# Fused attention and two feed-forward layers on one core: where the early stores are queued, and how soon the first layer's weights are asked for and decoded

## The chip, the cores and the metric

The kernel runs on one core of a Trainium2 chip. The metric is the device time of one execution in microseconds. Before the change three executions took 1014.46, 1020.41 and 1012.8 us, median 1014.46 us.

## The reference, cut to what matters

q, k, v and f are fp32, the weights arrive as 64-bit floats and are used as fp32. Attention over 4 batches and 8 heads of 576 tokens with head dimension 64, with a causal mask and a decay from running sums of log f; its output, 2304 tokens by 512, goes through two layers:

```
scores = q @ k.T / 8 + cum[:, None] - cum[None, :]      # masked above the diagonal
x = softmax(scores) @ v                                 # 4x8x576x64 -> 2304x512
h = x @ w_in;  g = h - tanh(h);   y = g @ w_out         # 2304x512x2048x512   (first layer)
h = y @ w2_in; g = relu(h)**2;    out = g @ w2_out      # the same sizes      (second layer)
```

## The kernel before, in words

**Matmuls in three products.** A fp32 matrix is split into a high part (fp32r) and the remainder, and a product is made of high x high, high x low and low x high. So every weight and every activation has to be split by the other engines before TensorE can take it.

**Weights.** The first layer's weights come in 16 chunks. Chunk fc is `wraw_fc` (512 KB of `w_in` and 512 KB of `w_out`, two DMAs on SyncE's queue, SP, through `load()`, L139). `decode_w()` (L185) makes fp32 of the 64-bit words and splits it, each in two halves: ACT scales the two words of each number (L203, L204), DVE puts their bits together (L210, L212, four instructions a chunk), ACT copies the high part (L227), and the low part is one subtraction for each half (L228): the first half on POOL, the second on DVE. A chunk thus issues five instructions on DVE (L210 twice, L212 twice, L228 once). `w_fc` is the result; TensorE needs it for `h` (L1007: x times `w_in`) and for `y` (L1047: g times `w_out`).

**Attention.** It goes by pairs of heads and halves of the queries: scores `s` (L701, L732), masks and decay on POOL (L543, from `neg`, rows of the running sums read back from `cscr` in DRAM), softmax on DVE and ACT (`Pb`, L661, L670), transposes `pt`, products `pv`, and the results `xt`. Two heads give `xs`; `pair_done()` (L876) splits it at once for the first block of 256 tokens, else it stores it to `xscr` in DRAM with `load()`, so on SP's queue and, while the early phase lasts, kept at its place in program order.

**First layer.** It runs by blocks of 256 tokens and by pairs of chunks of the hidden dimension: `h` on TensorE, tanh on ACT (L1017), `g = h - tanh(h)` on DVE (L1020), the high part `ghl` on ACT (L1024), the low part `ghl` on DVE (L1028), then `y`. `ghl_0_s` below is that of the first block's step s; step s takes the chunks 2s and 2s+1.

**What sets the order.** Attention's first pairs run alone; from the fifth pair on, attention's atoms and the first layer's steps are mixed by their costs (the loop at L1502 and on). All deferred work goes through `Clockwork`: `cw.later(k, fn)` runs fn k steps later, with k from the table `LAG` (L57). Weights are asked for by `feed.upload(n)` and decoded by `feed.pace(n)`. In the first pairs n comes from `UP[0] + i * UP[1]` and from `FEED[0]` to `FEED[1]` chunks; in the mixed part `paced()` sets them from the position in the first layer, with `UP[2]` as a factor for the asking, and the decoding is to reach 16 chunks at `FEED[2]` of a block's cost. When all 16 chunks have been asked for, `steady` is set and `load()` no longer keeps the program order.

The functions below carry the line numbers of the profile before; after the change all lines behind L141 stand six lower in the file (L228 is L234, L1007 is L1013, L1028 is L1034, L1047 is L1053).

Of the kernel before, what the change touches and what calls it, by code (L numbers as in the profile page):

```python
# [30 lines left out]
Q0, NQ, NK = (0, 256), (256, 320), (256, 576)  # L31
# [10 lines left out]
XB = (64, 768)  # L42
RING, WIDE = 5, 3
ENDS = (0.5, 1.0, 1.8, 6.45)
UP = (2, 0.1, 1.0)
HOT = 200
SUMS = 16

# [1 line left out]
NP2 = NF // 2  # L50
L2HOT = 200

FEED, FIRST = (1, 4, 0.7), 9


FILL = {2: 8, 4: 5}
LAG = dict(max=2, exp=1, norm=3, tr=3, trlo=2, pv=1, pvadd=1, qk=1, qklo=1, th=1, sub=1, hi=1, lo=1, wbits=2, wparts=3,  # L57
           relu=1, sq=1, lo2=1, load=8)


# [49 lines left out]
def fused_kernel(ctx: ExitStack, tc: tile.TileContext, q, k, v, f, w1i, w1o, w2i, w2o, out):  # L110
    nc = tc.nc
# [9 lines left out]
    xscr = {(b, hf): dram.tile([P, ND, NQ[hf]], F32, name=f"xscr_{b}_{hf}") for b in range(B) for hf in range(2)}  # L121
    yscr = [dram.tile([P, ND, NB], F32, name=f"yscr_{j}") for j in range(NBLK)]
    cscr = dram.tile([B * H, S], F32, name="cscr")
# [11 lines left out]
    steady = []  # L135

    def load(dst, src):

        ins = nc.sync.dma_start(dst, src)  # L139
        if not steady:  # L140
            tc.keep_in_program_order(ins)  # L141

    ordered = []

# [246 lines left out]
    def sum_logs(hf, tri, row, twice=None):  # L391

        s0, m = Q0[hf], NQ[hf]
        rps = bank("a", 4, f"rps_{hf}")
        chunks = [c for c, (k0, kn) in enumerate(KC) if k0 < s0 + m]
        for c in chunks:
            k0, kn = KC[c]
            lo = max(s0, k0)
            nc.tensor.matmul(rps[:32, lo - s0 : m], lhsT=lfT[:kn, c], rhs=tri_cols(tri, kn, lo - k0, s0 + m - lo),
                             start=c == 0, stop=c == chunks[-1])  # L400
        nc.vector.tensor_scalar(row[:, :m], rps[:32, :m], -8.0, None, op0=ALU.mult)
        (nc.sync if hf else nc.scalar).dma_start(cscr[:, s0 : s0 + m], row[:, :m])
        cps = bank("a", 4, f"cps_{hf}")
        for t in [c for c in chunks if KC[c][0] >= s0]:
            k0, kn = KC[t]
            for c in range(t + 1):
                cn = KC[c][1]
                o = min(k0 - KC[c][0], P)
                x = tri[:cn, o : o + P] if kn == P or c < t else twice
                nc.tensor.matmul(cps[:, t * 32 : t * 32 + 32], lhsT=x, rhs=lfT[:cn, c], start=c == 0, stop=c == t)  # L410
            nc.vector.tensor_scalar(ccol[:, t], cps[:, t * 32 : t * 32 + 32], 8.0, None, op0=ALU.mult)

    def first_sums():
# [5 lines left out]
        load_next("v")  # L419
        feed.upload(UP[0])  # L420
        make_identity(nc, ident)
# [219 lines left out]
    def softmax_of(i):  # L641
# [13 lines left out]
        def softmax(work):  # L655
# [11 lines left out]
            def ex():  # L667
                for x, (T, parts) in enumerate(work):
                    d = pb[:rows, T[2] : T[2] + T[3]]
                    soon(i, nc.scalar.activation(d, d, AF.Exp, bias=stat(len(parts) - 1, x)[:rows], scale=-1.0,  # L670
                                                 accum_out=stat(2, x)[:rows]))
                cw.later(LAG['norm'], nrm)

# [202 lines left out]
    def pair_done(b, hf, p, xs):  # L876
        if (b, hf) == (0, 0):
            t = xhl[0][p]
            nc.scalar.activation(t[:, 0], xs[:, :NB], AF.Copy)
            nc.vector.tensor_tensor(t[:, 1], xs[:, :NB], t[:, 0].bitcast(F32), op=ALU.subtract)  # L880
        else:
            load(xscr[b, hf][:, p, :], xs[:, : NQ[hf]])

    def attn_stream():

        yield 0, first_sums, 0
        yield 0, (lambda: (decay(0), decay(1), feed.upload(UP[0]))), 0
        for c, a in kq_atom(0):
# [568 lines left out]
    for i in range(n_start):  # L1457
        cw.step(astream[i][1], HOT)
        feed.upload(int(UP[0] + i * UP[1]))
        if i >= FIRST:  # L1460
# [16 lines left out]
    def paced():  # L1477
        if feed.loaded == NF and not steady:
            steady.append(True)
        if feed.loaded < NF:  # L1480
            feed.upload(min(NF, int(loaded0 + UP[2] * (NF - loaded0) * mpos / (FEED[2] * bc))))
        feed.pace(FEED[1] + (NF - FEED[1]) * mpos / (FEED[2] * bc) if feed.decoded < NF else goal2[0])
# [54 lines left out]
```

## Time and profile before

| | us |
|---|---|
| three executions | 1012.8, 1014.46, 1020.41 |
| the profiled execution | 1012.92 |
| its span | 1011.2 |
| TensorE busy in the span | 984.8 (97%) |
| VectorE (DVE) busy | 719.8 (71%) |
| ScalarE (ACT) busy | 629.3 (62%) |
| GpSimd (POOL) busy | 347.3 (34%) |

The profiled execution's time lies 1.72 us above its span. PE is TensorE, PEld its weight load. A TensorE that waits is idle; it can also be busy at half the clock, and then the same matmuls take twice as long, so both are to be read: the idle time of a stretch and its granted clock.

### The profile page before, as it was taken

What the parts mean: (1) busy time and instruction counts of PE and PEld (TensorE: products, weight loads), DVE (VectorE), ACT (ScalarE), POOL (GpSimd) and SP (SyncE); (2) the same over time, 40 slices, a digit from 0 to 9 for tenths busy, and PEclk for the clock granted to TensorE, in tenths of its full rate; (3) what the DMA queues carried; (4) which work ended last, traced back from release to release, by engine and by line L of the source; (5) the groups of instructions that cost most, each with busy time, mean ns of one, the idle gap of its engine ahead of it and who ended that gap; (6) DMA issues with size and microseconds to landing.
All of it is one profiled execution on the core that took longest, in us unless ns stands there. A gap on an engine that the chain in (4) does not pass through costs nothing.

```text
span 1011.2 us, 19924 instructions
## 1 busy us (share of the span) xinstructions
PE 984.8 (97%) x7022; PEld 938.4 (93%) x7022; DVE 719.8 (71%) x1497; ACT 629.3 (62%) x1249; POOL 347.3 (34%) x513
## 2 busy tenths in 40 slices
PE   7979999999999999999999999999999998999998
PEld 5768889999999999999999877999999998999998
DVE  4797884587787887878653488855447579888773
ACT  5786874566666666666543367766567777565651
POOL 3554452464555655555520243342333000000000
PEclk9799999999999999999999999999999999999999
DMA  8946645354353453444200532476876974544431
GB/s 235 271 128 198 219 114 122 80 137 89 73 137 90 100 125 80 96 119 97 67 14 27 167 125 84 148 263 222 282 272 246 331 230 132 147 143 130 125 106 42
DMA packets 217444, 146.96 MB, mean 145 GB/s; under 512 B 115872, under 2 KB 195040, under 8 KB 217344
## 3 DMA queue, kind: packets, MB, share of 16 engines
q1 hardware_dynamic: 217296, 145.65, 49.5%
q8 instruction: 55, 0.90, 0.4%
q14 instruction: 45, 0.37, 0.1%
q10 hardware_dynamic: 48, 0.03, 0.0%
HBM read 101.00 MB, written 39.92 MB: 139 GB/s over the span
## 4 chain that ended last, share of the span: by engine, by line
PE 73%; DVE 6%; ACT 3%; issue 2%; DMA 2%; SPq 1%; POOL 0%; ACTq 0%; DVEq 0%
PE h L1007 16%; PE y L1047 16%; PE o L1374 15%; PE r L1216 14%; PE pv L848 3%; PE pt L765 3%; PE s L733 2%; PE s L732 2%; DMA wscr<-wfull 1%; DVE PT L775 1%; PE pv L810 1%; DVE g L1020 1%; DVE wq L313 1%; SPq L150 1%; DVE ghl L1028 1%
## 5 line engine op out<-in xcount | busy, mean ns | idle before, releaser
L1047 PE MATMUL y<-ghl,w 128*128 128x256 f32 (+1 forms) x1536 | 242.0, 302 | 1.5 <-DVE ghl L1028 1.5
L1047 PEld LDWEIGHTS y<-ghl,w 128*128 128x128 f32 x1536 | 210.7, 192 | 13.8 <-DVE ghl L1028 3.3
L1007 PE MATMUL h<-x,w 128*128 128x256 f32 x1344 | 198.3, 290 | 6.7 <-POOL w L228 5.4
L1007 PEld LDWEIGHTS h<-x,w 128*128 128x128 f32 x1344 | 175.7, 192 | 13.3 <-POOL w L228 7.2
L1374 PE MATMUL o<-ws,gc 128*128 128x256 f32 x864 | 116.4, 283 | 0.0
L1374 PEld LDWEIGHTS o<-ws,gc 128*128 128x128 f32 x864 | 109.3, 192 | 0.0
L1216 PE MATMUL r<-yt,ws 128*128 128x384 f32 x576 | 106.2, 336 | 0.8 <-ACT g L1234 0.8
L1216 PEld LDWEIGHTS r<-yt,ws 128*128 128x128 f32 x576 | 100.0, 188 | 2.8 <-ACT g L1234 2.2
L1374 PE MATMUL o<-wq,gc 128*128 128x256 f32 x648 | 91.7, 284 | 3.1 <-DVE gc L1340 2.5
L1374 PEld LDWEIGHTS o<-wq,gc 128*128 128x128 f32 x648 | 83.8, 192 | 4.1 <-DVE gc L1340 3.1
L686 POOL TENSOR_SCALAR Pb<-Pb,st 128x384 f32<-128x384 f32 (+2 forms) x80 | 54.4, 680 | 92.2 <-DVE st L680 81.9
L661 DVE CUSTOM_DVE_ANT_0 Pb<-s,Pb 128x256 f32<-128x256 f32 (+4 forms) x144 | 66.9, 481 | 25.2 <-PE s L733 16.2
L1340 DVE TENSOR_TENSOR gc<-graw,gc 128x1792 fp32r<-128x1792 f32 x34 | 68.7, 2024 | 20.6 <-ACT gc L1339 20.5
L670 ACT ACTIVATE Pb<-Pb,st 128x384 f32<-128x384 f32 (+2 forms) x80 | 55.2, 690 | 44.5 <-DVE st L661 43.5
L1216 PE MATMUL r<-yt,wq 128*128 128x384 f32 x432 | 80.0, 335 | 0.1
L1020 DVE TENSOR_TENSOR g<-h,g 128x512 f32<-128x512 f32 x72 | 49.3, 685 | 38.8 <-ACT g L1017 37.9
L1339 ACT ACTIVATE gc<-graw 128x1792 fp32r<-128x1792 f32 x34 | 57.7, 1698 | 30.8 <-PE o L1374 19.5
L1216 PEld LDWEIGHTS r<-yt,wq 128*128 128x128 f32 x432 | 75.1, 188 | 1.1 <-ACT g L1234 0.9
L256 POOL TENSOR_TENSOR wsum<-wfull 128x256 f32<-128x256 f32 x32 | 30.0, 937 | 118.7 <-DVE wfull L212 96.8
L1227 DVE TENSOR_TENSOR g<-r,g 128x384 f32<-128x384 f32 x71 | 39.1, 554 | 42.3 <-PE r L1216 21.0
L775 DVE TENSOR_TENSOR PT<-pt,PT 128x512 fp32r<-128x512 f32 (+1 forms) x80 | 50.7, 634 | 24.4 <-ACT PT L774 16.3
L1024 ACT ACTIVATE ghl<-g 128x512 fp32r<-128x512 f32 x72 | 45.2, 628 | 34.9 <-DVE g L1020 34.4
(159 smaller groups left out, 1891.7 us busy)
## 6 DMA issues: line engine op xcount, KB each, us to landing
graw<-gscr SPq DMA_DIRECT2D x144, 128.0 KB, 2.6
gscr<-g SPq DMA_DIRECT2D x95, 192.0 KB, 4.1
wraw<-in_moe_w_in_dram SPq DMA_DIRECT2D x32, 512.0 KB, 4.6
wraw<-in_moe_w_out_dram SPq DMA_DIRECT2D x32, 512.0 KB, 5.9
neg<-cscr SPq DMA_DIRECT2D x32, 288.0 KB, 3.7
v<-in_v_dram SPq DMA_DIRECT2D x48, 128.0 KB, 2.8
qk<-in_k_dram SPq DMA_DIRECT2D x64, 72.0 KB, 2.4
K<-K SPq DMA_DIRECT2D x32, 144.0 KB, 3.3
```

Source lines behind the costliest of these rows:

```text
L661: soon(i, nc.vector.tensor_tensor_reduce(out=d, in0=t[:rows, src : src + m], in1=d, scale=-0.125, scalar=3.0e38 if j == 0 else stat(0, x)[ ...
L670: soon(i, nc.scalar.activation(d, d, AF.Exp, bias=stat(len(parts) - 1, x)[:rows], scale=-1.0, accum_out=stat(2, x)[:rows]))
L686: nc.gpsimd.tensor_scalar(d, d, r, 1.0, op0=ALU.mult, op1=ALU.mult)
L775: cw.later(LAG['trlo'], lambda: nc.vector.tensor_tensor(dst[1], src, dst[0].bitcast(F32), op=ALU.subtract))
L1007: nc.tensor.matmul(o, lhsT=win(fc, wh, dc), rhs=xpart(j, dc, xh), start=dc == 0 and wh + xh == 0, stop=dc == ND - 1 and wh == 1)
L1020: pin(nc.vector.tensor_tensor(g, t, g, op=ALU.subtract))
L1024: pin(nc.scalar.activation(ghl[:, 0], g, AF.Copy))
L1047: nc.tensor.matmul(o, lhsT=wout(fc, wh, i * P, P), rhs=ghl[:, xh, fj * n : fj * n + n], start=s == 0 and fj == 0 and wh + xh == 0 and i % ...
L1216: nc.tensor.matmul(t, lhsT=wprod(1, p, k, wh)[:, dc * P : (dc + 1) * P], rhs=yt[i, k][:, xh, dc], start=k in FRESH and dc == 0 and wh + xh ...
L1339: pin(nc.scalar.activation(hi, t[:, 1:8], AF.Copy))
L1340: pin(nc.vector.tensor_tensor(lo, in0=t[:, 1:8], in1=hi.bitcast(F32), op=ALU.subtract))
L1374: nc.tensor.matmul(o, lhsT=gc[n][gh, e][:, GWHERE[k]] if n == 1 else gc[n][gh][:, GWHERE[k], e], rhs=wprod(2, 2 * q + e, k, wh), start=q = ...
```

## The change

Three numbers and a queue. `UP[2]` goes from 1.0 to 2.5: in the mixed part the chunks are asked for 2.5 times as fast. `FEED` goes from (1, 4, 0.7) to (1, 6, 0.6): six instead of four chunks are to be begun by the end of the first pairs, and all at 0.6 instead of 0.7 of a block's cost. `LAG['wbits']` goes from 2 to 1 and `LAG['wparts']` from 3 to 1: DVE's bits follow ACT's first step by one step, and the split follows the bits by one. A new `store()` puts attention's stores to `xscr` on ScalarE's queue as long as chunks are still to be asked for, and on SP's afterwards; the second store of the running sums to `cscr` goes to ScalarE's queue, too.

```diff
-UP = (2, 0.1, 1.0)
+UP = (2, 0.1, 2.5)
-FEED, FIRST = (1, 4, 0.7), 9
+FEED, FIRST = (1, 6, 0.6), 9
-LAG = dict(..., wbits=2, wparts=3,
+LAG = dict(..., wbits=1, wparts=1,

+    def store(dst, src):
+        if steady:
+            nc.sync.dma_start(dst, src)
+        else:
+            tc.keep_in_program_order(nc.scalar.dma_start(dst, src))

 def sum_logs(hf, tri, row, twice=None):
-        (nc.sync if hf else nc.scalar).dma_start(cscr[:, s0 : s0 + m], row[:, :m])
+        nc.scalar.dma_start(cscr[:, s0 : s0 + m], row[:, :m])

 def pair_done(b, hf, p, xs):
-            load(xscr[b, hf][:, p, :], xs[:, : NQ[hf]])
+            store(xscr[b, hf][:, p, :], xs[:, : NQ[hf]])
```

**SP, behind chunk 6's weights.** `wraw` are the weights, `xscr` the stores of attention's results, `cscr` that of the running sums, `neg` their reading back. Before:

```order
L139 DMA wraw_6_716<-in_moe_w_out_dram 128x1024
L139 DMA qk_755<-in_k_dram 128x4x64 x2
L139 DMA qk_755<-in_q_dram 128x4x64 x2
L139 DMA xscr_0_71<-xs_772 128x256
L139 DMA wraw_7_798<-in_moe_w_in_dram 128x4x256
L139 DMA wraw_7_798<-in_moe_w_out_dram 128x1024
L139 DMA neg_806<-cscr 128x2x256
L139 DMA wraw_8_884<-in_moe_w_in_dram 128x4x256
L139 DMA wraw_8_884<-in_moe_w_out_dram 128x1024
L402 DMA cscr<-early_119 32x320
```

and in the changed kernel:

```order
L139 DMA wraw_6_680<-in_moe_w_out_dram 128x1024
L139 DMA wraw_7_732<-in_moe_w_in_dram 128x4x256
L139 DMA wraw_7_732<-in_moe_w_out_dram 128x1024
L139 DMA wraw_8_754<-in_moe_w_in_dram 128x4x256
L139 DMA wraw_8_754<-in_moe_w_out_dram 128x1024
L139 DMA wraw_9_788<-in_moe_w_in_dram 128x4x256
L139 DMA wraw_9_788<-in_moe_w_out_dram 128x1024
L139 DMA qk_797<-in_k_dram 128x4x64 x2
L139 DMA qk_797<-in_q_dram 128x4x64 x2
L139 DMA wraw_10_807<-in_moe_w_in_dram 128x4x256
L139 DMA wraw_10_807<-in_moe_w_out_dram 128x1024
L139 DMA neg_848<-cscr 128x2x256
```

The 36 rows ahead of these read alike in both. Behind them the weights of chunks 7 to 15 now follow with no store between them. Two stores to `xscr` and the one to `cscr` go to ACT's queue; the later stores to `xscr` stand on SP again.

**DVE, ahead of the low half of the second step, `ghl_0_1`** (L1028; L1034 in the changed kernel). L210 and L212 are bits and L228 a split of chunk `wfull_n`/`w_n`; `Pb` and `sp` are attention's softmax. Before:

```order
L1028 TENSOR_TENSOR ghl_0_0_699<-g_0_0_698,ghl_0_0_699 128x512
L679 TENSOR_SCALAR sp_106<-sp_106 128x4
L1020 TENSOR_TENSOR g_0_1_762<-h_0_1_704,g_0_1_762 128x512
L680 RECIPROCAL sp_106<-sp_106 128x4
L210 SCALAR_TENSOR_TENSOR wfull_6_765<-wfull_6_765 128x512
L661 ISA Pb_102,sp_107<-s_844,Pb_102 128x256
L661 ISA sp_107 128x1
L212 SCALAR_TENSOR_TENSOR wfull_6_765<-wfull_6_765 128x512
L210 SCALAR_TENSOR_TENSOR wraw_6_716<-wraw_6_716 128x512
L1028 TENSOR_TENSOR ghl_0_1_763<-g_0_1_762,ghl_0_1_763 128x512
```

and in the changed kernel, from the same `g_0_1` on:

```order
L1026 TENSOR_TENSOR g_0_1_804<-h_0_1_738,g_0_1_804 128x512
L234 TENSOR_TENSOR w_5_629<-wfull_5_598,w_5_629 128x512
L218 SCALAR_TENSOR_TENSOR wfull_6_683<-wfull_6_683 128x512
L216 SCALAR_TENSOR_TENSOR wraw_6_680<-wraw_6_680 128x512
L667 ISA Pb_102,sp_107<-s_887,Pb_102 128x256
L667 ISA sp_107 128x1
L218 SCALAR_TENSOR_TENSOR wfull_6_683<-wraw_6_680 128x512
L216 SCALAR_TENSOR_TENSOR wfull_7_735<-wfull_7_735 128x512
L216 SCALAR_TENSOR_TENSOR wraw_7_732<-wraw_7_732 128x512
L218 SCALAR_TENSOR_TENSOR wfull_7_735<-wfull_7_735 128x512
L234 TENSOR_TENSOR w_6_710<-wfull_6_683,w_6_710 128x512
L218 SCALAR_TENSOR_TENSOR wfull_7_735<-wraw_7_732 128x512
```

The next row of the changed kernel is `ghl_0_1`'s low half. So chunk 6 is split and chunk 7's bits are done ahead of it. Counted in DVE's program order, the decoding instructions (80 in all, five a chunk) that stand ahead of the low half of `ghl_0_s` are:

| s | 0 | 1 | 2 | 3 | 4 | 5 | 6 | 7 |
|---|---|---|---|---|---|---|---|---|
| before | 29 | 32 | 44 | 52 | 63 | 66 | 73 | 80 |
| changed | 29 | 39 | 54 | 63 | 73 | 80 | 80 | 80 |

Ahead of row 101 of DVE's order, the softmax of the scores `s_682` (`s_715` in the changed kernel), late in the first pairs, there are 17 of them in both.

**PE, ahead of the first `y` of `ghl_0_1`.** Before, `h_0_2` of chunk 5 is followed by `y`:

```order
L1007 MATMUL h_0_2_861<-x_0_125,w_5_779 128x256 x3
L1007 MATMUL h_0_2_861<-x_1_126,w_5_779 128x256 x3
L810 MATMUL pv_887<-v_512,PTF_117 128x64 x6
L1007 MATMUL h_0_2_861<-x_2_127,w_5_779 128x256 x3
L1007 MATMUL h_0_2_861<-x_3_128,w_5_779 128x256 x3
L1047 MATMUL y_0_0_787<-ghl_0_1_763,w_2_435 128x256 x3
```

and in the changed kernel:

```order
L1013 MATMUL h_0_2_904<-x_2_127,w_5_629 128x256 x2
L1013 MATMUL h_0_2_904<-x_3_128,w_5_629 128x256 x3
L1013 MATMUL h_0_3_1081<-x_0_125,w_6_710 128x256 x3
L1013 MATMUL h_0_3_1081<-x_1_126,w_6_710 128x256 x3
L1013 MATMUL h_0_3_1081<-x_2_127,w_6_710 128x256 x3
L1013 MATMUL h_0_3_1081<-x_3_128,w_6_710 128x256 x2
L1053 MATMUL y_0_0_831<-ghl_0_1_805,w_2_365 128x256
```

The `h` of chunk 6 now stands ahead of that `y`. Counted in matmuls from the start, the first `h` of chunk 6 moves from 314 to 268 and that of chunk 12 from 541 to 491; the first `y` of `ghl_0_1` moves from 274 to 279, that of `ghl_0_4` from 495 to 496. From the 696th matmul on the two orders are the same but for two small swaps. That matmul ran at 142.5 us before.

## Rows read from the trace of the kernel before

**Rows 1.** Page, part 1: busy us, share of the span, instructions by engine.

```profile
PE 984.8 (97%) x7022; PEld 938.4 (93%) x7022; DVE 719.8 (71%) x1497; ACT 629.3 (62%) x1249; POOL 347.3 (34%) x513
```

**Rows 2.** Stretches (us): length, busy by engine (instructions), granted clock, DMA share, GB/s.

```profile
25.90:36.00 10.10, 10.10 (x39) 8.00 (x38) 4.66 (x18) 5.42 (x17) 4.75 (x10) 0.50 0.98 242
36.00:45.70 9.70, 9.22 (x73) 7.34 (x72) 8.58 (x32) 8.74 (x29) 7.34 (x15) 1.00 1.08 324
45.70:65.20 19.50, 13.91 (x88) 11.59 (x88) 19.45 (x37) 16.12 (x36) 9.80 (x12) 0.95 0.39 98
65.20:112.10 46.90, 45.51 (x313) 39.87 (x313) 40.17 (x88) 36.94 (x88) 22.20 (x26) 0.94 0.61 188
112.10:142.50 30.40, 28.73 (x226) 26.42 (x225) 25.30 (x61) 24.43 (x61) 16.51 (x23) 0.96 0.72 208
142.50:1011.20 868.70, 857.23 (x6189) 830.83 (x6187) 610.59 (x1226) 524.17 (x987) 276.74 (x397) 1.00 0.47 136
```

**Rows 3.** Waits, 36 to 142.5 us: total us, times, longest.

```profile
POOL w L228 <- ACT w L227: 32.9, 13, 5.6
ACT w L227 <- DVE wfull L212: 8.0, 9, 2.3
POOL Pb L543 <- DMA neg<-cscr: 5.8, 3, 4.1
PE h L1007 <- POOL w L228: 5.4, 7, 1.2
PE h L1007 <- ACT w L227: 1.2, 2, 0.9
ACT wfull L203 <- DMA wraw<-in_moe_w_out_dram: 0.4, 1, 0.4
```

**Rows 4.** Waits of SP's queue, 36 to 142.5 us.

```profile
SPq L139 <- ACT xs L831: 40.5, 5, 15.4
SPq L402 <- DVE early L401: 8.8, 1, 8.8
```

**Rows 5.** Timeline of SP's queue: start us, us, issue.

```profile
65.74 0.34 SPq L139 DMA_DIRECT2D xscr<-xs  x1
```

**Rows 6.** Decoding by line and form, 45.7 to 142.5 us: busy us, mean ns.

```profile
L228 POOL TENSOR_TENSOR w<-wfull,w 128x512 fp32r<-128x512 f32 x14 | 20.4, 1454 | 30.6 <-ACT w L227 30.6
L228 DVE TENSOR_TENSOR w<-wfull,w 128x512 fp32r<-128x512 f32 x14 | 15.4, 1098 | 1.4 <-ACT w L227 1.4
L212 DVE SCALAR_TENSOR_TENSOR wfull<-wraw 128x512 uint32<-128x512 uint32 x14 | 11.5, 820 | 0.0
L212 DVE SCALAR_TENSOR_TENSOR wfull<-wfull 128x512 uint32<-128x512 uint32 x14 | 11.3, 805 | 0.1
L210 DVE SCALAR_TENSOR_TENSOR wraw<-wraw 128x512 uint32<-128x512 uint32 x14 | 10.8, 773 | 0.0
L210 DVE SCALAR_TENSOR_TENSOR wfull<-wfull 128x512 uint32<-128x512 uint32 x14 | 10.0, 711 | 0.8 <-ACT wfull L204 0.8
```

**Rows 7.** Timeline of DVE: start us, us, instruction.

```profile
68.86 0.68 DVE L1028 TENSOR_TENSOR ghl<-g,ghl 128x512 fp32r<-128x512 f32 x1
...
111.47 0.68 DVE L1028 TENSOR_TENSOR ghl<-g,ghl 128x512 fp32r<-128x512 f32 x1
```

**Rows 8.** Timeline of PE: the first `y` of the second and fifth step.

```profile
72.52 0.76 PE L1047 MATMUL y<-ghl,w 128*128 128x256 f32 x5
...
112.36 0.63 PE L1047 MATMUL y<-ghl,w 128*128 128x256 f32 x2
```

**Rows 9.** Timeline of POOL: a mask behind a late `neg`.

```profile
73.45 3.04 POOL L543 TENSOR_SCALAR Pb<-neg,ccol 128x128 f32<-128x128 f32 x3 [0.61 <-DMA neg<-cscr]
```

**Rows 10.** Stretches at half the clock, columns as in rows 2.

```profile
63.20:66.60 3.40, 3.40 (x18) 3.39 (x18) 3.40 (x9) 3.02 (x7) 0.28 (x1) 0.53 0.00 1
87.60:90.70 3.10, 3.10 (x16) 3.10 (x16) 1.38 (x4) 2.00 (x7) 0.00 (x0) 0.50 1.01 276
111.40:114.80 3.40, 3.40 (x19) 3.40 (x19) 1.90 (x7) 2.37 (x9) 1.17 (x3) 0.53 0.99 289
```

More of the change, by code (lines that the diff above doesn't have):

```diff
@@ L51 @@
 L2HOT = 200
-FEED, FIRST = (1, 4, 0.7), 9
+FEED, FIRST = (1, 6, 0.6), 9
 FILL = {2: 8, 4: 5}
-LAG = dict(max=2, exp=1, norm=3, tr=3, trlo=2, pv=1, pvadd=1, qk=1, qklo=1, th=1, sub=1, hi=1, lo=1, wbits=2, wparts=3,
+LAG = dict(max=2, exp=1, norm=3, tr=3, trlo=2, pv=1, pvadd=1, qk=1, qklo=1, th=1, sub=1, hi=1, lo=1, wbits=1, wparts=1,
            relu=1, sq=1, lo2=1, load=8)
```

## The prediction

> **What bounds the kernel now.** The page's busy times come first: TensorE is busy for 984.8 of 1011.2 us, DVE for 71% [rows 1]. So only PE's idle 26.4 us and what it runs at half the clock can be won; work on the other engines costs something only where PE then waits.
>
> The order of the instructions says which stretch the change can reach. PE's matmuls run in the same order, but for two swaps, from the 696th on, which ran at 142.5 us, and SP's queue reads alike through chunk 6's weights, which it issued up to 45.5 us. Behind 142.5 us PE is busy for 857.23 of 868.70 us [rows 2], and I let that stretch stand. What is in play is 45.7 to 142.5 us, to which the view by stretches gives three parts [rows 2]: PE is idle for 5.59 us up to 65.2, for 1.39 us up to 112.1 and for 1.67 us up to 142.5. In the first part DVE is busy for 19.45 of 19.50 us; in the second it has 6.73 us free. DVE is the engine behind PE's waits there: the view of waits says that PE waits 5.4 us for POOL's half of a split and 1.2 us for ACT's high part, that POOL waits 32.9 us for ACT, and ACT 8.0 us for DVE's bits [rows 3].
>
> The clock is the second thing to read: in three stretches of 3.1 to 3.4 us PE ran at a granted clock of 0.50 to 0.53, so at the lower of its two levels, 1.2 GHz [rows 10]. At full clock they would have taken 1.60, 1.55 and 1.60 us less, 4.75 us in all.
>
> **The change, part by part.**
>
> *The stores on ACT's queue, and the weights asked for early.* In the trace of before, SP stood for 15.4 us at a store to xscr until ACT had its xs, and issued it at 65.74 us [rows 4, 5]; then it stood for 8.8 us at the store to cscr until DVE was done. The weights of chunks 7 and 8 waited behind these. Both blocks go. But what waited for the weights? ACT's first step waited for a weight DMA for 0.4 us once, and PE is in no row of the waits with one [rows 3]. So the earlier weights by themselves are worth 0 to 0.4 us: **0**. The reverse side is what now stands behind 9 MB: one neg behind chunk 10, the next behind chunk 15. POOL waited for neg for 5.8 us already, with the mask at 73.45 us as one place [rows 3, 9]. At the 324 GB/s moved from 36 to 45.7 us [rows 2], the 4 MB of chunks 7 to 10 take 12.9 us, so from 45.5 us that neg is in by 60 us and the second, behind another 5 MB, by 77. The first is before its time, the second is the one used later. Cost 0; from 0 to the rate at which it would decide, under rivals. On ACT each of the three stores is one more issue, 0.34 us as SP's [rows 5], in all 1.0 us on an engine 62% busy [rows 1]. ACT can also be held at the cscr store until DVE has written it. Bounds 0 and the 8.8 us for which SP stood there; I take 0 for PE, since ACT comes to that row only after work that SP didn't have ahead of it, and put 3 us of it into the slow case.
>
> *FEED and LAG: the order on DVE.* This is where the sum is made. Five instructions decode a chunk on DVE. Their 14 each from 45.7 to 142.5 us took 15.4, 11.5, 11.3, 10.8 and 10.0 us [rows 6], 59.0 in all: 4.2 us a chunk, 0.84 us an instruction. Ahead of the low half of ghl_0_s stand 39, 54, 63, 73 and 80 of them for s of 1 to 5, where there were 32, 44, 52, 63 and 66. The first step's count is 29 in both, and 17 stand in both ahead of the late pair's softmax, so "six chunks in the first pairs" does not show on DVE, and I let the time up to 65.2 us stand as well.
>
> - s = 1. The low half ended at 69.54 us [rows 7]. Seven more instructions are 5.9 us: 75.4. PE began that y at 72.52 us [rows 8]. In the new order it comes to it 5 matmuls later in count, but has been spared waits on the way; I take 72.1 to 72.5 us. It then waits for **3 us**, in place of 0.
> - s = 2 and 3. Ten and eleven more instructions are 8.4 and 9.2 us, less what is left to DVE of its 6.73 us idle by then; PE comes 3 us later as well. Bounds 0 and 0.8 us of further waits, I take 0.4.
> - s = 4. The half ended at 112.15 us [rows 7], and PE took it at 112.36 [rows 8]. Ten more instructions are +8.4 us; some 1.2 us of attention's work moves behind it in DVE's order (an estimate from the order and the means of its lines); DVE's 6.73 us idle are used up: 112.6 us. PE's matmuls up to this y are as many as before, by kind some 1.2 us less work (an estimate likewise); without the 1.39 us of old waits it would come at 109.8, with 3.4 us of new ones at 113.2. So both come together, and PE is **+0.8** behind before.
>
> - From there to the common point PE has the same 200 matmuls. They took 30.4 us, 28.73 of them busy [rows 2]. All decoding stands ahead of s = 5 now, so the 1.67 us of idle time go: **-1.67**. The half clock at 111.4 to 114.8 us I leave in, since PE may still wait just ahead of it: up to 2.8 us, if the earlier waits fail to come.
>
> On DVE's price of 0.84 us bears the collision with POOL: the splits on DVE have a mean of 1098 ns where the bits have 711 to 820, and POOL's splits one of 1454 ns [rows 6]. The 4.2 us a chunk hold the collisions that happened, and I keep them.
>
> By the Trainium skill, SBUF — State Buffer, Terms, DVE and POOL share a pair of ports that is locked for a whole instruction, and the loser blocks entirely. By that rule a chunk could cost DVE, besides five instructions at the lowest mean, POOL's whole split: 3.55 + 1.45 = 5.0 us (an estimate from this page), and the half of s = 4 would come 1.6 us later, the sum to +0.6. The trace bears the lock out only in part, since a mean of 1098 ns is not one of 711 and 1454 together.
>
> *Early clock.* From 25.9 to 36 us the clock was 0.50 for 10.1 us [rows 2], ahead of the change's first moved row on SP, but LAG acts there. Bounds: 5.05 us given back, or another 3.4 us at half clock, 1.7 us lost. I take 0, as DVE's counts there are equal.
>
> The sum: 0 + 0.8 - 1.67 + 0 = -0.9 us on the profiled execution's 1012.92, so 1012.0. The median of the runs stands 1.5 us above that execution: 1013.5. Of the three runs two lie at or below the median by up to 1.7 us and one far above, so I say **1013 us**.
>
> **The rivals.**
>
> *The lead pays (faster).* If the chunks are all ready when PE comes to h, the waits for POOL's and ACT's splits go without coming back at y. For it: chunk 6's h stands ahead of that y, so PE has something else to do in the meantime; DVE's price falls to the bits' 711 ns where POOL does not collide. Against it: that same h needs chunk 6's split, which DVE does just ahead of the low half. The ceiling is 3.06 us of idle time behind 65.2 us and 4.75 us of half clock: 7.8 us, with a part of the 5.59 us ahead of it 9. So 1005.5 to 1010.5, at its middle 1008.
>
> *The low halves come too late (slower).* PE waits at s = 1 and again at s = 4, and each wait is followed by another stretch at half clock, as the 63.2 us stretch came behind idle time. Waits of 3.8 us, of which nothing is won back as DVE in turn waits for PE, two stretches at 1.6 us and 3 us of ACT at the cscr store, less the 1.67: +8.3 at most, +5 in the middle. On the median that is 1016 to 1022. It decides once DVE's instruction stays at 0.84 us or above and the half of s = 1 ends over 1 us behind PE's arrival.
>
> *neg behind the weights (slower).* If the queue moves less than some 150 GB/s from 45.5 us on (4.2 MB in 28 us), the first neg is later than the 73.45 us at which POOL took it, and POOL, then softmax, then PE wait: 4 MB at the 98 GB/s of the next stretch [rows 2] would be 43 us. That rate is what was asked for, not what the queue could move, so I give it little: +10 us, 1024.
>
> *The change does less than it says.* Only two stores to xscr leave SP, and DVE's count is 17 in both at the end of the first pairs. Then all falls to the noise, 1014; it is within the forecast's range.
>
> **How the numbers follow.** Forecast 0.55 (its own range 1010 to 1016.5), the lead pays 0.24, halves too late 0.17, neg 0.04. The range: 1005 holds nearly all of the faster case; 1020 leaves out the neg case and the upper part of the slow one: **1005 to 1020**. 1%, about 10 us, is what can be told from no change. Faster by more needs the whole ceiling and some of the early clock: 0.08. Slower by more: the neg case and the end of the other, 0.07. Within: 0.85.
>
> **What would show it.** Right: PE's rows of waits for L228's split on POOL shrink from 5.4 us, and a wait for DVE's ghl appears at the second step, near 72 to 75 us; the 696th matmul falls between 140 and 143 us; SP has no stand of 15.4 us. Wrong: no wait at ghl (the lead pays), half-clock stretches behind the new waits or ACT standing at its cscr store (slower), POOL waiting longer for neg, or a time behind the 696th matmul that differs by over 2 us from 868.7.

## The result, and the profile after

The changed kernel is **slower**: five executions took 1019.83 to 1029.47 us, median 1025.22, against 1013.22 us before (five executions, 1011.86 to 1020.41); ratio 1.0115 with a 95% interval of 1.009 to 1.0139, so 9 to 14 us. The forecast was 1013 us, its range ended at 1020. The profiled execution took 1025.22 us. One execution of e2 below (1030.59 us) ran in a slower state of the chip and is left out of all numbers.

The page's busy times after the change, to be held against [rows 1]:

```profile
span 1023.5 us, 19911 instructions
PE 987.4 (96%) x7022; PEld 939.9 (92%) x7022; DVE 719.4 (70%) x1497; ACT 631.3 (62%) x1249; POOL 353.4 (35%) x513
```

PE does the same 7022 matmuls in nearly the same busy time, and is idle for 36.1 us in place of 26.4. The stretches of [rows 2], and below them three stretches at half the clock (start and end in us, length, busy by engine with instructions, granted clock, DMA share, GB/s):

```profile
25.90:36.00 10.10, 10.06 (x62) 7.07 (x61) 7.83 (x26) 7.52 (x23) 6.01 (x11) 1.00 0.93 236
36.00:45.70 9.70, 9.49 (x66) 7.49 (x65) 8.70 (x31) 9.52 (x29) 8.74 (x16) 1.00 1.06 299
45.70:65.20 19.50, 13.78 (x88) 11.90 (x88) 18.83 (x36) 16.33 (x35) 9.95 (x11) 0.91 1.04 338
65.20:112.10 46.90, 41.73 (x302) 36.06 (x301) 44.20 (x86) 40.20 (x92) 25.96 (x27) 0.97 0.53 167
112.10:142.50 30.40, 30.40 (x209) 27.77 (x209) 21.35 (x57) 18.54 (x53) 15.67 (x25) 0.82 0.45 105
142.50:1023.50 881.00, 862.52 (x6209) 835.82 (x6208) 608.08 (x1226) 526.50 (x989) 277.14 (x396) 1.00 0.47 134
109.10:122.70 13.60, 12.29 (x49) 10.15 (x47) 13.25 (x26) 10.30 (x25) 10.07 (x9) 0.50 0.36 106
617.70:621.10 3.40, 3.40 (x10) 2.62 (x9) 2.66 (x5) 2.15 (x4) 0.00 (x0) 0.50 0.00 0
737.20:740.50 3.30, 3.30 (x12) 3.30 (x12) 0.98 (x2) 1.39 (x3) 2.61 (x5) 0.50 0.59 141
```

Two things stand out. From 65.2 to 112.1 us PE is idle for 5.17 us where it was 1.39, and from 109.1 us on it runs at half the clock for 13.6 us. And there are stretches at half the clock at 617 and 737 us, where the profile before has none: the loss is not only in the stretch that the forecast looked at.

Both kernels issue the same number of matmuls in nearly the same order, so they can be matched one by one. The numbers count all 7022 matmuls of the trace, in which the forecast's 696th, at 142.5 us, is about the 835th. Up to the 845th the orders differ in places, so there the k-th matmul is not always the same work; behind it they differ only near the 4830th and the 5180th. How much later (us) the k-th matmul starts than in the profiled execution before, for the changed kernel and for kernels of the experiments below:

| kernel | 100 | 150 | 625 | 700 | 1000 | 4200 | 4500 | 4800 | 5000 | 7000 | 1000 to 7000 |
|---|---|---|---|---|---|---|---|---|---|---|---|
| changed | +1.0 | -1.9 | +2.7 | +5.4 | +2.5 | +2.5 | +7.3 | +8.7 | +12.6 | +12.3 | **+9.8** |
| e1, late lags alone | +0.6 | +0.6 | +1.2 | +2.3 | +2.3 | +2.4 | +7.2 | +8.6 | +11.6 | +11.2 | **+8.9** |
| e2, changed without late lags | +0.7 | +3.1 | +10.3 | +12.7 | +9.9 | +9.9 | +9.9 | +9.9 | +10.7 | +13.0 | +3.1 |
| e5, first matrix | +0.9 | -3.5 | -3.5 | -3.5 | -3.5 | -3.5 | +1.4 | +2.8 | +2.5 | +3.6 | **+7.0** |
| e6, second matrix | +1.3 | +2.4 | +4.1 | +4.1 | +4.3 | +4.3 | +4.3 | +4.4 | +8.0 | +7.6 | **+3.4** |
| e7, late lag of the bits | +0.1 | +0.1 | +3.0 | +3.0 | +3.1 | +3.1 | +4.3 | +5.4 | +11.1 | +11.0 | **+7.9** |
| e8, late lag of the parts | +1.1 | +0.9 | -0.4 | -0.4 | 0.0 | 0.0 | +0.3 | +0.9 | +4.4 | +4.0 | **+4.0** |
| e15, UP alone | 0.0 | -4.4 | -6.8 | -5.1 | -6.5 | -6.4 | -6.4 | -6.4 | -6.3 | -6.0 | +0.4 |

In the changed kernel 2.5 us are lost by the 1000th matmul, nothing to the 4200th (572 us before), and 9.8 us behind it. The last column tells what a kernel loses late; in eleven kernels whose late orders are those of before it lies between -0.5 and +1.4 us, and in a twelfth (e2) at +3.1. What a single trace shows by the 1000th says little: e1 and e5 to e8 have the instructions of before in the same order on every engine up to 575 us, and lie there between -3.5 and +4.3. The difference is in the clock. The stretch from 25.9 to 142.5 us in before, e5 and e6, columns as in [rows 2]:

```profile
25.90:142.50 116.60, 107.47 (x732) 93.21 (x732) 98.15 (x229) 91.66 (x228) 60.61 (x84) 0.91 0.67 194
25.90:142.50 116.60, 105.39 (x766) 91.70 (x767) 99.44 (x245) 94.33 (x236) 63.90 (x86) 0.97 0.66 196
25.90:142.50 116.60, 105.62 (x703) 91.77 (x703) 93.26 (x225) 89.44 (x222) 60.42 (x81) 0.88 0.64 189
```

So the late loss can be read from a trace, and the early one only from the times of many executions.

**The late loss.** Waits of PE from 550 to 800 us (in total, times, longest), before:

```profile
PE y L1047 <- DVE ghl L1028: 1.5, 2, 0.9
PE r L1216 <- ACT g L1234: 0.8, 1, 0.8
```

and after:

```profile
PE y L1053 <- DVE ghl L1034: 5.0, 3, 2.3
PE r L1222 <- ACT g L1240: 3.9, 3, 2.3
```

The code says why: `decode_w()` serves the second layer's weights as well, and its two lags are read there for every phase. The second layer's chunks are decoded from 560 to 780 us, one behind the other, and shorter lags bring the next steps of the decoding up in DVE's and ACT's order. DVE ahead of the low half behind the longest wait for ghl, from its `g` on, and PE's `y` behind it. The same matmul, the 4359th, before:

```profile
606.82 0.68 DVE L1020 TENSOR_TENSOR g<-h,g 128x512 f32<-128x512 f32 x1
608.71 0.69 DVE L313 TENSOR_TENSOR ws<-wsum,ws 128x512 fp32r<-128x512 f32 x1 [1.22 <-ACT ws L312]
609.32 0.69 DVE L1028 TENSOR_TENSOR ghl<-g,ghl 128x512 fp32r<-128x512 f32 x1
```

```profile
610.06 2.79 PE L1047 MATMUL y<-ghl,w 128*128 128x512 f32 x11 [0.65 <-DVE ghl L1028]
```

and after:

```profile
611.47 0.68 DVE L1026 TENSOR_TENSOR g<-h,g 128x512 f32<-128x512 f32 x1
612.07 0.92 DVE L216 SCALAR_TENSOR_TENSOR wraw<-wraw 128x512 uint32<-128x512 uint32 x1
613.02 0.69 DVE L218 SCALAR_TENSOR_TENSOR wfull<-wraw 128x512 uint32<-128x512 uint32 x1
614.41 0.69 DVE L319 TENSOR_TENSOR wq<-wfull,wq 128x512 fp32r<-128x512 f32 x1 [0.70 <-ACT wq L318]
615.02 1.21 DVE L1034 TENSOR_TENSOR ghl<-g,ghl 128x512 fp32r<-128x512 f32 x1
```

```profile
616.29 3.94 PE L1053 MATMUL y<-ghl,w 128*128 128x512 f32 x11 [2.35 <-DVE ghl L1034]
```

Before, one split, `ws`, stood between g and the low half, with 1.22 us of waiting for ACT's high part. Now two bits instructions of a chunk and its split `wq` stand there, with 0.70 us of waiting, and the low half itself takes 1.21 us for 0.69. So it is done 4.8 us behind the start of its g where it was 3.2. PE waits 2.35 us in place of 0.65, and 1.4 us later the clock is at half. At the second place it is ACT, before:

```profile
727.41 0.66 ACT L203 ACTIVATE wfull<-wraw 128x512 uint32<-128x512 uint32 x1 [1.71 <-DMA wscr<-wfull]
...
728.52 0.48 ACT L1234 ACTIVATE g<-r 128x384 f32<-128x384 f32 x1
```

and after, with PE's r:

```profile
733.39 0.66 ACT L209 ACTIVATE wfull<-wraw 128x512 uint32<-128x512 uint32 x1 [3.62 <-DMA gscr<-g]
...
734.50 0.48 ACT L1240 ACTIVATE g<-r 128x384 f32<-128x384 f32 x1
```

```profile
735.03 1.33 PE L1222 MATMUL r<-yt,wq 128*128 128x384 f32 x6 [2.26 <-ACT g L1240]
```

ACT comes to the next chunk's first step earlier, stands there for a DMA (the profile names a store to wscr before, one to gscr after) for 3.62 us in place of 1.71, and the `g` that PE needs is behind it. Before, PE's r waited 0.81 us behind that step, and it was an r 24 matmuls further on in r's order; the r that waits now did not wait then, since its g stood ahead of the chunk's step.

**The early part.** Waits from 36 to 142.5 us after the change, for [rows 3]:

```profile
PE h L1013 <- POOL w L234: 3.6, 4, 1.2
PE xt L831 <- DVE xq L825: 2.2, 1, 2.2
PE h L1013 <- ACT w L233: 1.8, 1, 1.8
PE h L1013 <- DVE g L1026: 1.3, 1, 1.3
POOL Pb L549 <- DMA neg<-cscr: 0.2, 1, 0.2
```

The waits for POOL's splits shrink, as forecast. No y waits for ghl. In its place PE waits for `xq`, attention's result, which DVE did late:

```profile
107.90 0.44 PE L831 MATMUL xt<-ident,xq 128*128 128x128 f32 x2 [2.24 <-DVE xq L825]
```

In DVE's order 42, 56 and 69 decoding instructions now stand ahead of the three xq's in question, where there were 34, 45 and 55. The stretch of 13.6 us at half clock begins at 109.1 us, between this wait and the one for g. In e2, which has the changed kernel's order there, the same two waits (2.29 and 1.51 us) are followed by 6.8 us at half clock.

**SP still stands at the stores.** Waits of its queue, for [rows 4], and its timeline (start us, us, issue):

```profile
SPq L139 <- POOL Pb L549: 22.5, 6, 8.8
SPq L139 <- DMA xscr<-xs: 16.6, 2, 8.4
```

```profile
61.83 0.37 SPq L139 DMA_DIRECT2D neg<-cscr  x1
70.62 0.36 SPq L139 DMA_DIRECT2D wraw<-in_moe_w_in_dram  x1
...
80.18 0.37 SPq L139 DMA_DIRECT2D neg<-cscr  x1
88.81 1.09 SPq L139 DMA_DIRECT2D v<-in_v_dram  x2
```

and the two stores on ACT's queue:

```profile
67.96 0.35 ACTq L147 DMA_DIRECT2D xscr<-xs  x1
85.01 0.33 ACTq L147 DMA_DIRECT2D xscr<-xs  x1
```

The first row is of a later time: all weights are asked for by 79 us, and 21.9 of its 22.5 us lie behind 91.5. The second row is of the weights' time. The weights at 70.62 us have no data in common with the store at 67.96. But in the trace's operands the store sets semaphore 102 when it has landed, at 70.60 us, and these weights wait for 102 and then set it themselves. Here eight semaphores go round over the DMAs of both queues in program order, so a load that has its turn behind a store waits for that store wherever it is queued.

### The profile page after: what moved, and what is told of

It is laid out like the page before. It is cut to its first block, busy times and chain, and to the rows that moved or that the text cites. A ratio compares the mean times of both kernels' runs of the same rounds, so it can differ in the third digit from the quotient of the medians.

```text
span 1023.5 us, 19911 instructions
## 1 busy us (share of the span) xinstructions
PE 987.4 (96%) x7022; PEld 939.9 (92%) x7022; DVE 719.4 (70%) x1497; ACT 631.3 (62%) x1249; POOL 353.4 (35%) x513
## 4 chain that ended last, share of the span: by engine, by line
PE 71%; DVE 8%; ACT 4%; issue 3%; DMA 2%; SPq 1%; POOL 0%; DVEq 0%; ACTq 0%
PE y L1053 16%; PE h L1013 16%; PE o L1380 15%; PE r L1222 11%; PE pv L854 3%; PE pt L771 3%; PE s L739 2%; PE s L738 2%; PE pv L816 1%; DVE wfull L218 1%; DMA wscr<-wfull 1%; DMA gscr<-g 1%; DVE yt L1171 1%; PE s L707 1%; DVE PT L781 1%
## 5 line engine op out<-in xcount | busy, mean ns | idle before, releaser
L1034 DVE TENSOR_TENSOR ghl<-g,ghl 128x512 fp32r<-128x512 f32 x72 | 56.4, 783 | 16.1 <-ACT ghl L1030 15.9
```

The costliest lines, as they stand in the source:

```text
L1034: pin(nc.vector.tensor_tensor(ghl[:, 1], g, ghl[:, 0].bitcast(F32), op=ALU.subtract))
```

## The experiments

Each kernel ran 6 to 12 times beside 23 to 34 executions of the kernel before on the same chip, which had medians of 1012.9 to 1015.4 us. The edits are given against the kernel before, for e2 against the changed one; `phase` is 0 for the first layer's weights, 1 and 2 for the second layer's two matrices.

The executions of one kernel spread over 10 us, and most of it is the clock: over 126 executions of the kernel before (those beside e1 to e16), time and mean granted clock have a correlation of -0.89, a line through them falls by 7.8 us for 0.01 of clock, and the executions lie 1.3 us around it. The last column below is a kernel's mean distance from that line, so its time beside that of before at the same mean clock. It tells idle time from clock; it is no verdict, since a wait can bring the clock down too, and from one chip's executions to another's the kernel before itself lies between 1.0 us below the line and 0.6 above it.

| | kernel | ratio (95%) | mean clock | us at equal clock |
|---|---|---|---|---|
| | before | 1 | 0.9912 | 0 |
| | changed | 1.0115 (1.009 to 1.0139) | 0.9864 | +7.7 |
| e1 | late lags alone | 1.0073 (1.0049 to 1.0097) | 0.9881 | +5.7 |
| e2 | changed, old late lags | 1.0036 (1.0007 to 1.0065) | 0.9885 | +2.1 |
| e3 | early lags alone | 0.9988 (0.9964 to 1.0012) | 0.9907 | -1.3 |
| e4 | stores alone | 1.0032 (1.001 to 1.0054) | 0.9900 | +1.3 |
| e5 | late lags, first matrix | 1.0061 (1.0034 to 1.0087) | 0.9916 | +5.6 |
| e6 | late lags, second matrix | 1.0038 (1.0018 to 1.0059) | 0.9892 | +1.9 |
| e7 | late lag of the bits | 1.0079 (1.0051 to 1.0108) | 0.9889 | +5.6 |
| e8 | late lag of the parts | 1.0041 (1.0014 to 1.0067) | 0.9894 | +2.1 |
| e9 | UP, FEED, early lags | 1.0035 (1.0005 to 1.0065) | 0.9863 | -1.3 |
| e10 | FEED alone | 1.0034 (1.001 to 1.0058) | 0.9885 | +0.5 |
| e11 | stores and UP | 1.0029 (1.0009 to 1.005) | 0.9880 | -0.2 |
| e12 | early lags 1, late parts 4 | 1.0036 (1.0011 to 1.0061) | 0.9875 | -1.0 |
| e13 | FEED (1, 6, 0.7) | 0.999 (0.9965 to 1.0015) | 0.9912 | +0.8 |
| e14 | FEED (1, 4, 0.6) | 0.9967 (0.9946 to 0.9989) | 0.9916 | -2.4 |
| e15 | UP alone | **0.9936 (0.9912 to 0.996)** | 0.9933 | -3.1 |
| e16 | FEED (1, 4, 0.8), early lags 1 | 1.0031 (1.0013 to 1.005) | 0.9872 | +1.8 |
| e17 | UP and FEED | 1.0022 (0.9996 to 1.0049) | 0.9899 | -0.4 |
| e18 | UP and early lags | 1.0016 (0.9989 to 1.0043) | 0.9879 | -1.9 |

**e1 and e2: the lags of the second layer's weights, alone and taken out.**

```diff
 e1:
-            cw.later(LAG['wbits'], lambda: bits(x))
+            cw.later(1 if phase else 2, lambda: bits(x))
-                cw.later(LAG['wparts'], (lambda: parts(0)) ...
+                cw.later(1 if phase else 3, (lambda: parts(0)) ...
 e2 (on the changed kernel): 2 if phase else 1;  3 if phase else 1
```

> The kernel before with the lags of one step (bits and splits) for the second layer's weights alone; the first layer's weights keep 2 and 3, and nothing else is changed. Its orders are those of before up to the second layer's weights. Theory L (the loss behind 550 us comes of the second layer's decoding being taken up earlier on DVE and ACT, in front of what TensorE waits for): 9.8 us above before, about 1023 us, with waits of y for DVE's ghl of some 5 us between 585 and 620 us and r waiting for ACT's g near 665 and 730 us. Rival E (the late loss is a consequence of the early part, by a queue or a shifted phase): as before, 1013 us within 2 us. Rival N (the late waits differ from run to run): between, and a spread of 10 us.

> The changed kernel with the lags of 2 and 3 put back for the second layer's weights alone. Theory L: only the early loss is left, 2.5 us above before, about 1015.7 us, and behind 550 us the waits of before. Rival E: as the changed kernel, 1025 us.

Measured: 1022.17 us for e1 (ratio 1.0073) and 1018.61 us for e2 (1.0036). Both sides agree: put in alone the late lags cost 7.4 us (5.0 to 9.8), and taken out of the changed kernel they give back 8 us of its 11.6. From 550 to 800 us e1 has the changed kernel's three waits for ghl, and r's longest wait is shorter (1.4 for 2.3 us); e2 has the waits for ghl of before, and 0.8 us more for g. First e1, then e2:

```profile
PE y L1047 <- DVE ghl L1028: 5.1, 3, 2.3
PE r L1216 <- ACT g L1234: 3.1, 3, 1.4
```

```profile
PE r L1222 <- ACT g L1240: 1.6, 3, 0.9
PE y L1053 <- DVE ghl L1034: 1.5, 2, 0.9
```

In the table of matched matmuls e1 keeps its shift from the 1000th to the 4200th and then loses 8.9 us, as the changed kernel 9.8. Theory L holds, and rival E falls: e1's orders up to the second layer's weights are those of before. Rival N falls as far as the waits for ghl go: they are 1.3, 1.4 and 2.3 us long in the traces of the changed kernel, e1 and e5 alike. e2's median is 3 us above what was expected, with executions from 1011.57 to 1025.9.

**e5 to e8: which matrix, and which of the two lags.** The same two lines, with lags by phase (0, 1, 2):

```diff
 e5:  wbits (2, 1, 2)  wparts (3, 1, 3)
 e6:  wbits (2, 2, 1)  wparts (3, 3, 1)
 e7:  wbits (2, 1, 1)  wparts (3, 3, 3)
 e8:  wbits (2, 2, 2)  wparts (3, 1, 1)
```

> The kernel before with lags of one step for the decoding of the second layer's first matrix alone (its chunks are decoded at 560 to 640 us, while attention's tail and the last blocks of the first layer run). In the trace of the kernel with both late lags, TensorE's matmuls lost 4.9 us between the 4200th and the 4500th and 4.0 us behind that. Theory P1 (the splits of the weights go ahead of ghl's low half on DVE): 4.9 us above before, about 1019 us, three waits of y for ghl of 1.3 to 2.4 us, and half clock once. Rival P2 (it is the second matrix, on ACT): 0 to 1 us above.

> The same with lags of one step for the second layer's second matrix alone (decoded at 640 to 780 us). Theory P1: 4.0 us above before at most, about 1018 us, with r waiting for ACT's g near 655 and 725 us, where ACT stands at the first step of the next chunk until a store to wscr has landed. Rival P2: all of the 7.4 us that both together cost by the clock, 1021 us. A third way: no more than 1 us, if those waits need the shift that the first matrix brings.

> The kernel before with the lag of the bits at one step for both matrices of the second layer, the lag of the parts at 3 as before. If the waits come of the splits standing ahead of ghl (lag of the parts), this one is within 2 us of before; if they come of the bits, it has the 7.4 us. Both together shorten a chunk's chain from 2 x 2 + 3 to 2 x 1 + 1 steps, by 2 steps each, so by a theory in which only the chain's length counts each has about half, 3.7 us above.

> The counterpart: the lag of the parts at one step, that of the bits at 2 as before, for both matrices of the second layer. By the splits theory 5 to 7 us above before (1018 to 1021); by the bits theory within 2 us; by the chain's length 3.7 us above.

Measured: 1018.46, 1016.54, 1020.53 and 1017.06 us. Both matrices take part, the first with 6.2 us (3.4 to 8.8) and the second with 3.9 (1.8 to 6.0); matched matmul by matmul, 7.0 and 3.4 us. Together that is more than both lags cost in e1, within the intervals. Theory P1 holds for the place in e5, and in e6 for the wait near 725 us alone, not for the one near 655. The lag of the bits alone costs 8.0 us (5.2 to 10.9), as much as both lags, that of the parts 4.2 (1.4 to 6.8). The longest waits of PE from 550 to 800 us, e7 and below it e8:

```profile
PE r L1216 <- ACT g L1234: 4.7, 2, 3.9
PE r L1216 <- ACT g L1234: 3.4, 2, 3.2
```

In both, y waits for ghl for 0.5 us at most. With one lag short, the low half shown above has the split `ws` ahead of it as before and one or two bits instructions, and DVE does not stand idle there: that loss needs both lags. The long wait of r for ACT's g, near 730 us, comes with either lag alone. So the splits theory falls as worded: a split stood ahead of this low half before, too, and e8 does not have the waits for ghl. The chain's length does not set the price either: two steps less by the bits cost about twice what two less by the parts do, though the intervals overlap. Which of the two lags is the worse in the changed kernel stays open.

**e3 and e4: the early lags alone, the stores alone.**

```diff
 e3: wbits (1, 2, 2)  wparts (1, 3, 3)
 e4: store() and its call in pair_done(), cscr's second store on nc.scalar; nothing else
```

> The kernel before with the lags of one step for the first layer's weights alone; stores, asking and FEED as before. Theory S (in the early part the shorter lags spare the half clock at 26 to 36 us, and the run-ahead that costs more comes of FEED and of the early asking): 2 to 3 us below before, about 1010.5 us, clock 1.00 from 26 to 36 us. Rival R (the lags themselves put the decoding ahead of xq and of the low halves): 2 to 3 us above before, 1015 to 1016 us, with half clock near 110 us for over 10 us.

> The kernel before with the stores to xscr and the second store to cscr on ScalarE's queue alone. Theory (no wait of TensorE on weights or stores hangs on SP's stands): as before, 1013 us within 1.5 us, with SP's stand of 15.4 us gone. Rival (SP's stands did delay chunks 7 to 9, which DVE had free time to take earlier): 2 us below.

Measured: 1012.45 us for e3 (0.9988), 1015.78 us for e4 (1.0032). e3 can't be told from before; neither S nor R is shown. S's half about the clock falls: in e3's profiled execution, the slowest of its twelve, the clock is at half for 27.3 us from 25 us on. e2's trace has the same; e2's stretches are

```profile
25.90:36.00 10.10, 10.10 (x41) 7.39 (x42) 5.07 (x21) 5.61 (x18) 4.58 (x10) 0.58 0.86 224
36.00:55.00 19.00, 19.00 (x74) 14.99 (x74) 10.35 (x35) 10.49 (x33) 9.12 (x17) 0.51 0.69 195
```

while the changed kernel, whose instructions are in e2's order up to 575 us, was at 1.00 in both. The stores alone cost 3.2 us (1.0 to 5.5) where 0 was expected. SP's stand of 15.4 us is gone in e4's trace, but the queue now stands for 13.6 us until PE has done an `h`; where PE loses the 3.2 us isn't shown.

**e9 to e11: what of the early part.**

```diff
 e9:  UP = (2, 0.1, 2.5);  FEED = (1, 6, 0.6);  wbits (1, 2, 2)  wparts (1, 3, 3);  stores as before
 e10: FEED = (1, 6, 0.6)
 e11: UP = (2, 0.1, 2.5);  stores on ScalarE's queue
```

> The changed kernel without its stores on ScalarE's queue (they stand on SP's as before) and with the old lags for the second layer's weights: so UP, FEED and the first layer's lags alone. The version with the stores as well stood 3.6 us above before, and the stores alone 3.2 us. Theory Q (of the early part the stores are what costs): as before within 1.5 us, 1013 us. Rival F (FEED's and UP's run-ahead costs, through xq and g behind the decoding on DVE): 3 to 4 us above before, 1017 us.

> The kernel before with FEED at (1, 6, 0.6) alone. Theory Q: as before, 1013 us within 1.5 us. Rival F: 2 to 4 us above, with TensorE waiting for xq near 106 us as in the changed kernel.

> The stores on ScalarE's queue together with UP at 2.5, all else as before: stores and early asking as they are meant to go together. Theory Q: 3 us above, 1016 us, as with the stores alone. Rival: the early asking sets the store's early phase to an end sooner and takes it back: 1013 us.

Measured: 1017.52, 1016.69 and 1016.35 us, all some 3 us above before. Theory Q (the stores alone are to blame) falls with e9 and e10. Rival F has the size of both, but its mechanism is not shown: in e9's trace PE waits 3.0 us for xq, in e10's not at all (its waits are for the splits on POOL and ACT). At equal clock the three lie at -1.3, +0.5 and -0.2 us: by that measure PE doesn't wait longer in sum, it runs longer at half clock.

**e13, e14, e16: does the decoding ahead of xq set the price?** FEED's two numbers apart, and a slower decoding.

```diff
 e13: FEED = (1, 6, 0.7)
 e14: FEED = (1, 4, 0.6)
 e16: FEED = (1, 4, 0.8);  wbits (1, 2, 2)  wparts (1, 3, 3)
```

> Of FEED only the six chunks begun in the first pairs, (1, 6, 0.7). Ahead of the xq's of the mixed part, in DVE's order, stand 34, 45, 54, 63 decoding instructions, against 34, 45, 55, 64 before. Theory X (the early part's cost goes with the decoding that stands ahead of xq, g and the low halves): as before, 1013 us within 1.5 us. Rival B (any other order of the early part costs some 3 us, since the one before was the best of many): 1016 us.

> Of FEED only the 0.6 of a block's cost, (1, 4, 0.6). Ahead of the same xq's stand 34, 52, 59, 69. Theory X: 2 to 4 us above before, 1016 us, as with both numbers of FEED. Rival (it is the six chunks): 1013 us.

> The opposite direction: FEED at (1, 4, 0.8), so that the first layer's weights are decoded later, with the first layer's lags at one step; stores, UP and the second layer as before. Ahead of the same xq's stand 34, 44, 50, 59, fewer than before. Theory X: 1 to 3 us below before, 1011 us. Rival B: 1016 us. A third way: the chunks come late for h, which waits for POOL's and ACT's splits, 2 to 5 us above.

Measured: 1012.62, 1010.48 and 1018.25 us. Theory X falls in both directions: e14, with up to seven instructions more ahead of xq, is faster (0.9967), and e16, with fewer, is slower (1.0031), by its third way: from 66 to 142 us PE waits there 3.3 us for ACT's high part and 3.1 us for POOL's splits, where it was 0.3 and 2.6. Rival B falls too, as e13 and e14 are not 3 us above.

**e15, e17, e18: asking early alone, and with one of the others.**

```diff
 e15: UP = (2, 0.1, 2.5)
 e17: UP = (2, 0.1, 2.5);  FEED = (1, 6, 0.6)
 e18: UP = (2, 0.1, 2.5);  wbits (1, 2, 2)  wparts (1, 3, 3)
```

> UP at 2.5 alone. Ahead of the same xq's stand 34, 48, 55, 67; the stores keep SP standing, so that the early asking can't run ahead of them. Theory X: 0 to 2 us above before, 1014 us. Rival B: 1016 us.

> UP at 2.5 and FEED at (1, 6, 0.6) together, all else as before. Ahead of the low halves of steps 1 to 5 stand 39, 51, 62, 74, 80 decoding instructions, as in the changed kernel (39, 54, 63, 73, 80); with UP alone, which was 6 us below before, 32, 44, 53, 64, 74. Theory X (the decoding that stands ahead of the low halves and xq costs): 3 us above before, 1016 us, as the version with the first layer's lags besides (1.0035). Rival: that version's loss came of the lags, and this one is at 0.994, 1007 us.

> UP at 2.5 and the first layer's lags at one step, FEED and all else as before. Ahead of the low halves of steps 1 to 5 stand 33, 44, 55, 63, 73, nearly as with UP alone. Theory X: as UP alone or better, 1006 to 1009 us. Rival: the lags spoil it, 1016 us.

Measured: 1008.62 us for e15, 1014.24 and 1014.89 for the others. **UP alone beats both kernels**, 0.9936 of before (6.5 us, 4.1 to 8.9), by six executions on one chip, another chip than e11, e17 and e18 ran on. Theory X and rival B both fall with it; in e17 theory X's 3 us lie within the interval and the rival's 0.994 does not, in e18 it is the rival that the lags spoil it. In e15's profiled execution SP's queue stands, from 36 to 142.5 us, at the stores for

```profile
SPq L139 <- ACT xs L831: 32.0, 6, 12.3
```

so for as long as before [rows 4] in all but 8.5 us; PE is idle for 1.1 us from the 66th us to the 800th matmul where it was 2.5, and up to that matmul the clock is at half for 6.8 us where it was 20.5 (10.2 of these at 26 us). That clock proves little, since e5, with the order of before, also had only 6.8 us at half there. Adding FEED, the early lags or the stores (e11) takes the gain back each time. Of that the runs show the size, not the place.

**e12: longer lags.** `wbits (1, 2, 2), wparts (1, 4, 4)`.

> A version that goes the other way: the first layer's lags at one step, as in the changed kernel, and the second layer's lag of the parts at 4 in place of 3 (bits at 2), stores, UP and FEED as before. If the late waits shrink as the lag grows, the 2.3 us that TensorE still waits there in the kernel before (1.5 for ghl, 0.8 for g) go, and with the 1.2 us of the early lags it is 3 us below before, 1010 us. If 3 was already the best place, it is 0 to 4 us above.

Measured: 1015.67 us, 1.0036. So the late part is no better at 4: by matched matmuls it loses 0.8 us, which lies within what kernels with the late order of before show, and has a wait of r of 1.44 us at 652 us that before hasn't. At 1 it is worse (e8).

## Why the prediction was wrong, step by step

- **"Behind 142.5 us PE is busy for 857.23 of 868.70 us, and I let that stretch stand."** This is the step that failed. It rested on PE's order, which is the same there but for two swaps. But what a matmul waits for is the order on DVE and ACT, and that was moved again from 575 us on, by the same two numbers of LAG. It cost 7.4 us (e1) of the 11.6. In the profiled execution the changed kernel loses 9.8 us there, far over the 2 us that the forecast itself named as a sign of being wrong: waits of some 6.6 us more, and two stretches of 3.4 us at half clock that lose 1.7 us each. With 7.4 us in the sum, -0.9 would have been +6.5, and the range, moved as far, would have held the time.
- **"The stores on ACT's queue": "Both blocks go."** They went, but others came in their place: SP stood for 8.4 us twice, until the stores on the other queue had landed. The size put on it for PE was 0; alone the stores cost 3.2 us (e4).
- **neg behind 9 MB: 0.** Right. POOL waited for neg for 0.2 us, down from 5.8.
- **The order on DVE, s = 1 to 4.** The prices were right: the changed kernel's decoding took 4.25 us a chunk on DVE (forecast 4.2), and between the low halves of steps 0 and 1 lie 9.6 us where there were 4.3, so 5.4 more (forecast 5.9). By the Trainium skill, SBUF — State Buffer, Terms, the loser of the port pair that DVE and GpSimd share blocks for the whole instruction. The forecast's estimate by that was 5.0 us a chunk, and the trace goes with the row's 4.2. (A half 1.6 us later would have made that sum +0.7 at most, not +0.6.) The waits were wrong: the low half of s = 1 ended at 72.74 us and that of s = 4 at 113.38, PE began their y's at 72.80 and 113.46, and no idle time of PE lies ahead of them. The 3 us at s = 1 did not come. What came late was `xq`, with 8 to 14 more instructions ahead of it, and `g`: 2.24 and 1.31 us of waits. The forecast counted DVE's order ahead of one tile only.
- **From s = 4 to the common point: -1.67.** The idle time did go: PE is busy for 30.40 of 30.40 us. But it ran at a clock of 0.82, and at the common point, 142.5 us before, the changed kernel was 2.5 us behind in place of 0.9 ahead.
- **Early clock: 0.** In the profiled execution 10 us at half clock were spared, worth 2.9 us by matched matmuls. That was one execution's luck: e2, with the same order there, had 27.3 us at half. Without it this execution would have been some 5.4 us behind at the common point (an estimate, 2.5 and 2.9).
- **The rivals.** The slower one came nearest: waits, the longer ones followed by half clock. Its place was wrong (not the low halves at s = 1 and 4, not ACT at the cscr store), and the measured time lies above its 1016 to 1022.

What is shown: the late lags cost some 7 us, by e1 and e2 from both sides, in two places seen in the trace. What stays open: of the other 3.6 us (0.7 to 6.6), which of stores, FEED and early lags makes how much. UP alone gains; UP with any one of the three is at or above before; the stores alone and FEED alone each lose some 3 us, FEED's two numbers apart lose nothing, and the 0.6 even gains 3.3 us (1.1 to 5.5). The measurements don't add up part by part, and by the table's last column the difference is in the clock more than in the waits.

## What to carry to other kernels

When a change turns a number that several stages read, look for all its readers, and compare the order of every engine to the program's end: an unchanged order on the bounding engine doesn't mean unchanged waits. Moving a store to another queue frees a queue only if what comes next doesn't wait for the store by a semaphore that goes round over both. And a package of small settings should be timed one by one: here one of them alone was 6 us faster, and the package 12 us slower.

## What the runs showed of the hardware

- The clock early in the program is not set by the order of instructions alone. The changed kernel and e2 are alike up to 575 us, and up to 55 us their profiled executions were at half for nothing and for 27.3 us. Before, e1 and e5 to e8 are alike up to 575 us, and from 25 to 142.5 us they were at half for 6.8 us (e5) to 27.3 us (e6). Over the executions of the kernel before the mean granted clock runs from 0.984 to 0.997, and accounts for most of a spread of over 10 us.
- Behind 550 us a wait of 2.3 us for ghl was followed by 3.4 us at half clock in three traces (changed, e1, e5); a wait of 2.1 us for g by 3.4 us (e6), one of 3.2 us, still going on when the clock fell, by 3.4 us (e8), and one of 3.9 us, also still going on, by 6.8 us (e7). The waits of up to 1.4 us for ghl ahead of these were not.
- Two queues' DMAs were held together by a semaphore that both use in turn: the load at 70.62 us followed 0.02 us behind the landing, at 70.60 us, of a store on the other queue.
